# Two-stage attention and a squared-ReLU MLP on one core: a seventh group of seven-product block multiplies, products added inside PSUM, weight differences moved to GpSimd

## The chip, the cores and the metric

The kernel runs on one core of one Trainium2 chip. The core's engines run side by side and meet at semaphores: TensorE (PE in the profile; PEld is its weight loads), VectorE (DVE), ScalarE (ACT), GpSimd (POOL) and SyncE (SP). Each engine works through its own list of instructions in order. Matrix products land in PSUM; DVE and ACT carry them from there to SBUF. The metric is the time of one execution on the device in microseconds, taken as the median of several runs.

## The reference

For each of 8 batches and 8 heads there are 576 tokens of 64 numbers (q, k, v) and 32 pack vectors p. Two attentions follow one another, and an MLP takes the heads of a token side by side as 512 numbers:

```python
def sm_attn(qq, kk, vv):
    s = scale * np.matmul(qq, kk.transpose(0, 1, 3, 2))
    s = s - np.max(s, axis=-1, keepdims=True)
    a = np.exp(s)
    a = a / (np.sum(a, axis=-1, keepdims=True) + 1e-09)
    return np.matmul(a, vv)
p_packed = sm_attn(p, k, v)
out = sm_attn(q, p_packed, p_packed)
...
x = np.ascontiguousarray(attn_out.transpose(0, 2, 1, 3)).reshape(B * S, H * D)
h = x @ w_in          # 4608 x 512 times 512 x 2048
r = np.maximum(h, 0.0)
return ((r * r) @ w_out).astype(np.float32)   # 4608 x 2048 times 2048 x 512
```

## The kernel before, in words

**Stages of a batch.** For batch b the kernel transposes k (Tk), forms the pack scores on PE (S1), takes their maxima on DVE (MX) and exponentials on ACT (EX), transposes them (E, EC) and multiplies with v (PV). The packed vectors are normalised (RC, XN) and, instead of being carried through the second attention, multiplied with w_in first: four products M of 512 columns each, copied to SBUF by MC. The second attention's scores come from S2; SI transposes them, SM, SU, SE, SS, SN and SO are its softmax (maxima, subtraction, exponential, sum, scaling, transposition). F1 (for batches 0 and 1 cut in pieces, F) multiplies the probabilities with M and gives h transposed, 128 of its 2048 features at a time; R takes the ReLU out of PSUM, SQ (or Q) squares it into the tile `gT`.

**The last product.** `gT` holds the squared values of two batches. The product with w_out runs over tiles of 128 tokens, numbered 0 to 35. A plain tile (F2, lines 907 to 911) is 16 matmuls of 512 columns that add up in one PSUM bank, one copy (FC) and a store (ST). Where four whole tiles lie in a batch, they can be a group: 512 tokens times 2048 features times 512 columns is cut into 2 by 2 blocks, and seven block products replace eight. Groups exist for batches 2 to 7. Each product GP.z.g (z = 0 to 6, group g, two halves of eight matmuls of 256 columns, line 975) needs block sums: GS.0 to GS.3 are sums of squared values for each group (line 963), WS.0 to WS.3 differences of blocks of w_out, made once (line 956, two halves each, so 8 instructions of 1,024 columns). The seven products take turns in two PSUM banks (`OUTS`); GC carries them to the output tile `o_sb`: one copy and seven additions that read `o_sb` and PSUM (line 994).

**What sets the order.** A planner written in the kernel (`Plan.forward`) lists every piece of work with its engine, its length and what it needs, and lays the pieces out by priorities. A table of numbers, found by search, shifts the priorities (`TABLE`, 'o') and the choice between ACT and DVE (`TABLE`, 'l'), so that the order of each engine's list is fixed when the program is built. Before the first F2, PE's gaps are filled with products of a zero tile that nobody reads (`keep_clock`, line 590). Inputs are loaded by POOL's DMA queue in the order of the string `ORDER`; each load waits until the eighth load before it has landed (line 1018). Batches 5, 6 and 7 are transposed by DMA from SP's queue once the loads are through; SP also issues nearly all stores.

The pieces that the change touches: GROUPS (line 223), `w_sum` (952), `gp_mm` (967), `g_copy` and `g_add` (987, 991), the GC list (from 1253), the WS pieces (1230), and the tile 'e1T' that EC and the DMA transposes write.

Of the kernel before, what the change touches and what calls it, by code (L numbers as in the profile page):

```python
# [41 lines left out]
class Plan:  # L42
# [6 lines left out]
    def add(self, *a, **kw):  # L49
        self.pieces.append(Piece(*a, **kw))  # L50
# [169 lines left out]
ORDER = "k0 v0 x0 a0 y0 a1 a2 a3 k1 b0 b1 v1 b2 q1 b3 b4 b5 b6 b7 k2 v2 q2 k3 v3 q3 k4 v4 q4 k5 v5 q5 k6 v6 q6 k7 v7 q7"  # L220

KHW = 2
GROUPS = (2, 3, 4, 5, 6, 7)
XBAR = (5, 6, 7)

TABLE = {'o': {'Lk.0.0i': -10.9333, 'Lk.0.1i': -54.9223, 'Lk.0.0': 47.5347, 'LP.0': -80.9731, 'Lk.0.1': -9.0183, 'I2':
# [270 lines left out]
def kernel_impl(tc, q, k, v, p, w_in, w_out, out):  # L497
# [23 lines left out]
    with ExitStack() as ctx:  # L521
# [213 lines left out]
        def s1_tr(b, qd, u):  # L735
            t = pst[b, qd] = half(u[0]).bitcast(BF16)[:, :(GM + 1) * P]
            for g in range(GM + 1):
                c0 = g * P if g < GM else S - P
                nc.tensor.transpose(t[:, g * P:(g + 1) * P], e1[:, qd, c0:c0 + P], ident[:])
# [615 lines left out]
```

## Time and profile before

| | before |
|---|---|
| median of 3 runs | 237.85 us (237.77 to 238.49) |
| the profiled execution | 238.34 us, of which the span of its instructions is 236.6 us |
| PE busy | 225.6 us, 95% of the span |
| DVE busy | 202.5 us, 86% |
| ACT busy | 157.2 us, 66% |
| POOL busy | 59.2 us, 25%, all but one instruction of it in the first 113 us |
| granted PE clock over the span | 0.99 |

PE's busy time is 95% over the whole span, but that is an average over parts that differ: a beginning in which PE waits for loads and a chain of softmax steps, a long middle in which it hardly pauses, and an end that is the last copy and store. DVE is nearly as full as PE between 40 and 200 us. The profiled execution took 238.34 us, 0.49 us more than the median, so sums that are made against it are carried over to the median as differences.

### The profile page before, as it was taken

Reading aid. Unit: us, or ns where it says so; the run is one execution under the profiler, and the core shown is the slowest. Engines: PE = TensorE matmul, PEld = TensorE weight load, DVE = VectorE, ACT = ScalarE, POOL = GpSimd, SP = SyncE. Lnnn points to the kernel's source line nnn. Section 1 sums busy time; section 2 is a strip of 40 time slices with the busy share of each in tenths; the row PEclk is TensorE's granted clock in tenths of the full one; section 3 lists DMA queues with packets and bytes.
Section 4 is the critical chain, followed back from the end, with each engine's and each line's share of the span. In section 5 each row is a group of like instructions: output and inputs, shape, how many; then the busy total and the mean of one; then the engine's idle time right before and its main releaser. Section 6 shows DMA issues by size and latency. Waiting matters only on the chain.

```text
span 236.6 us, 6395 instructions
## 1 busy us (share of the span) xinstructions
PE 225.6 (95%) x2636; PEld 160.2 (68%) x2636; DVE 202.5 (86%) x340; ACT 157.2 (66%) x245; POOL 59.2 (25%) x106
## 2 busy tenths in 40 slices
PE   8888899999999999999999999999999999999991
PEld 5556655346544457857788877777848888888880
DVE  3669977997989999999998889999999999849550
ACT  3314987279959889899787834766977999516000
POOL 9787555333344657600000000000000000000000
PEclk9979999999999999999999999999999999999999
DMA  7999999999999999957596989738501003305216
GB/s 228 173 194 182 205 209 202 201 198 260 229 212 219 214 237 198 197 75 144 94 126 144 183 97 195 169 59 157 125 3 44 3 1 89 91 0 131 71 22 177
DMA packets 46764, 34.06 MB, mean 144 GB/s; under 512 B 25392, under 2 KB 38448, under 8 KB 46736
## 3 DMA queue, kind: packets, MB, share of 16 engines
q0 software_dynamic: 19408, 17.90, 47.2%
q1 hardware_dynamic: 26496, 14.98, 29.5%
q10 hardware_dynamic: 832, 0.79, 1.1%
q8 instruction: 20, 0.33, 0.6%
q14 instruction: 8, 0.07, 0.1%
HBM read 37.22 MB, written 9.44 MB: 197 GB/s over the span
## 4 chain that ended last, share of the span: by engine, by line
PE 82%; DVE 12%; ACT 2%; issue 1%; ACTq 1%; DVEq 0%
PE pb L975 31%; PE ps L857 20%; PE pb L911 8%; PE ps L885 6%; PE ps L911 4%; PE ps L783 3%; PE pb L590 2%; PE ps L706 1%; DVE wS L956 1%; PE ps L800 1%; DVE s L821 1%; ACTq L923 1%; ACT e L733 1%; DVE m L827 1%; DVE s L831 1%
## 5 line engine op out<-in xcount | busy, mean ns | idle before, releaser
L867 ACT ACTIVATE r_b<-ps 128x576 bf16<-128x576 f32 x80 | 46.8, 672 | 14.8 <-PE ps L857 14.2
L857 PE MATMUL ps<-a,M 128*128 128x288 bf16 x384 | 52.7, 286 | 0.0
L857 PEld LDWEIGHTS <-M 128*128 128x128 bf16 x384 | 37.2, 98 | 9.9 <-issue 0.2
L975 PEld LDWEIGHTS <-gT 128*128 128x128 bf16 x384 | 37.2, 98 | 6.4 <-issue 1.1
L584 ACT CAST M<-ps 128x1024 bf16<-128x1024 f32 (+1 forms) x33 | 29.8, 945 | 16.3 <-PE ps L783 16.2
L994 DVE TENSOR_TENSOR o_sb<-o_sb,pb 128x512 f32<-128x512 f32 x42 | 28.0, 676 | 8.3 <-PE pb L975 7.4
L911 PE MATMUL pb<-w_out_b,gT 128*128 128x512 bf16 x128 | 34.3, 380 | 0.1
L975 PEld LDWEIGHTS <-gS 128*128 128x128 bf16 x288 | 27.5, 98 | 5.5 <-issue 1.9
L923 POOL DMA_DIRECT2D out_dram<-o_sb x1 | 0.6, 577 | 118.7 <-issue 118.7
L911 PEld LDWEIGHTS <-gT 128*128 128x128 bf16 x176 | 15.8, 98 | 17.5 <-issue 4.0
L875 ACT ACTIVATE gT<-r_b 128x1152 bf16<-128x1152 bf16 x21 | 24.2, 1176 | 0.4 <-DVE r_b L869 0.2
L975 PE MATMUL pb<-wS,gS 128*128 128x256 bf16 x192 | 24.0, 273 | 0.0
L975 PE MATMUL pb<-wS,gT 128*128 128x256 bf16 x192 | 23.6, 273 | 0.0
L975 PE MATMUL pb<-w_out_b,gT 128*128 128x256 bf16 x192 | 23.6, 273 | 0.0
L893 ACT ACTIVATE r_b<-ps 128x512 bf16<-128x512 f32 (+2 forms) x27 | 16.8, 654 | 6.5 <-PE ps L885 6.5
L877 DVE TENSOR_TENSOR gT<-r_b 128x1152 bf16<-128x1152 bf16 x27 | 19.6, 747 | 1.6 <-ACT r_b L867 1.6
L885 PE MATMUL ps<-a,M 128*128 128x256 bf16 (+3 forms) x160 | 18.9, 262 | 1.9 <-DVE a L848 0.9
L885 PEld LDWEIGHTS <-M 128*128 128x128 bf16 x160 | 13.9, 97 | 6.8 <-issue 2.6
L584 ACT COPY o_sb<-pb 128x512 f32<-128x512 f32 (+1 forms) x14 | 7.9, 565 | 15.1 <-PE pb L929 12.6
L733 ACT ACTIVATE e<-ps,n 128x576 bf16<-128x576 f32 x16 | 11.8, 738 | 8.4 <-DVE n L725 7.0
L590 PE MATMUL pb<-zero 128*128 128x256 bf16 x92 | 15.2, 332 | 1.1 <-DVE zero L593 1.1
L834 ACT ACTIVATE e<-s 128x1152 bf16<-128x1152 f32 (+4 forms) x11 | 10.1, 917 | 7.0 <-DVE s L831 6.9
(92 smaller groups left out, 341.4 us busy)
## 6 DMA issues: line engine op xcount, KB each, us to landing
out_dram<-o_sb SPq DMA_DIRECT2D x65, 128.0 KB, 2.6
kq_b<-in_k_dram POOLq DMA_DIRECT2D x14, 288.0 KB, 10.1
kq_b<-in_q_dram POOLq DMA_DIRECT2D x10, 288.0 KB, 6.1
w_in_b<-in_moe_w_in_dram POOLq DMA_DIRECT2D x16, 128.0 KB, 5.7
w_out_b<-in_moe_w_out_dram POOLq DMA_DIRECT2D x8, 256.0 KB, 9.2
v_b<-in_v_dram POOLq DMA_DIRECT2D x5, 320.0 KB, 10.5
v_b<-in_v_dram POOLq DMA_DIRECT2D x12, 128.0 KB, 8.2
v_b<-in_v_dram POOLq DMA_DIRECT2D x5, 256.0 KB, 11.0
```

Of the source, the lines that this page charges most:

```text
L584: nc.scalar.copy(dst, src)
L590: nc.tensor.matmul(half(7)[:, :2 * P], lhsT=zero[:, :P], rhs=zero, start=True, stop=True)
L733: nc.scalar.activation(e_out(qd) if b in XBAR else e1[:, qd, :S], ps1[b, qd], ACT.Exp, bias=n1[b % 2][:, qd:qd + 1], accum_out=d1[b % 2][: ...
L857: nc.tensor.matmul(t[:, c], lhsT=M[b % 2][:, qd, fb * FB:(fb + 1) * FB], rhs=a2[b % 2][:, qd, c * HALF:(c + 1) * HALF], start=(qd == 0), s ...
L867: nc.scalar.activation(dst, src, ACT.Relu)
L875: nc.scalar.activation(dst, r, ACT.Square)
L877: eng.tensor_tensor(out=dst, in0=r, in1=r, op=ALU.mult)
L885: nc.tensor.matmul(t[:, c, m * w:(m + 1) * w], lhsT=M[b % 2][:, qd, fb * FB:(fb + 1) * FB], rhs=a2[b % 2][:, qd, o:o + w], start=(qd == 0) ...
L893: nc.scalar.activation(dst, ph["h", b, x, j], ACT.Relu)
L911: nc.tensor.matmul(po[t], lhsT=gT[:, fb, n0:n0 + P], rhs=w_out_b[:, fb, :], start=(fb == 0), stop=(fb == NFB - 1))
L975: nc.tensor.matmul(pz[g, k][:, i], lhsT=a[:, f, i * P:(i + 1) * P], rhs=w[:, f], start=(h == 0 and f == 0 and i == 0), stop=(h == 1 and f ...
L994: nc.vector.tensor_tensor(out=oC(g, i, j), in0=oC(g, *src), in1=pz[g, z], op=op)
```

## The change

- `GROUPS` gets batch 1: tiles 5, 6, 7 and 8 become a group of seven products in place of four plain tiles. Tiles 0 to 4, 13, 22 and 31 stay plain.
- Products 2, 3, 5 and 6 of a group no longer start a new sum in a PSUM bank. They add to the bank that already holds product 0, 1, 3 or 4 (`ON`), after GC has read it. The bank's readers so become two copies (GC.0, GC.2) and five additions in place of one copy and seven additions. The sign of WS.3 is turned around so that all of them add.
- The eight differences WS go from DVE to POOL, into the queue that issues the loads: two by two they stand behind the first load of q for batch 2 (four), between the two loads of k for batch 4 and behind the second (two), and among the loads of batch 4's q and behind batch 5's k (two).
- `e1T` becomes part of the tile `e1`, and the zero tile of `keep_clock` lies in a slot of `o_sb`.
- The table of priorities is a new one throughout, so the order of all engines' lists is another; PE's list has 112 matmuls of 256 columns more, 64 of 512 columns less, and 92 fillers as before.
- New tokens in `ORDER`, `XTURN` and `quiet` change nothing with the values given; the planner's lengths for the DMA transposes go from 2.0 and 3.4 to 1.6 and 2.9.

```diff
-GROUPS = (2, 3, 4, 5, 6, 7)
+GROUPS = (1, 2, 3, 4, 5, 6, 7)
 XBAR = (5, 6, 7)
+XTURN = (5, 6, 7)
...
-        zero = consts.tile([P, 2 * P], BF16, name="zero")
...
-        e1f = consts.tile([P, NQD * (GM + 1) * P + D], BF16, name="e1")
+        e1f = consts.tile([P, 2 * NQD * (GM + 1) * P], BF16, name="e1")
...
-        e1T = consts.tile([P, NQD, GM + 1, P], BF16, name="e1T")
+        e1T = e1f[:, NQD * (GM + 1) * P:].rearrange("p (q g n) -> p q g n", q=NQD, n=P)
...
+        zero = o_sb[:, 0, :P].bitcast(BF16)
...
-            a, b = ((wB(0, 1, hs), wB(0, 0, hs)), (wB(1, 1, hs), t[0]), (wB(1, 1, hs), wB(0, 1, hs)), (t[1], wB(1, 0, hs)))[i]
-            nc.vector.tensor_tensor(out=t[i], in0=a, in1=b, op=ALU.subtract)
+            a, b = ((wB(0, 1, hs), wB(0, 0, hs)), (wB(1, 1, hs), t[0]), (wB(1, 1, hs), wB(0, 1, hs)), (wB(1, 0, hs), t[1]))[i]
+            nc.gpsimd.tensor_tensor(out=t[i], in0=a, in1=b, op=ALU.subtract)
...
+        ON = {2: 0, 3: 1, 5: 3, 6: 4}
         def gp_mm(g, k, h, u=None):
-            if u is not None:
-                pz[g, k] = half(u[0]).rearrange("p (i n) -> p i n", i=2)
+            if h == 0:
+                pz[g, k] = pz[g, ON[k]] if k in ON else half(u[0]).rearrange("p (i n) -> p i n", i=2)
...
-                                     start=(h == 0 and f == 0 and i == 0), stop=(h == 1 and f == HB // 2 - 1 and i == 1))
+                                     start=(k not in ON and h == 0 and f == 0 and i == 0), stop=(h == 1 and f == HB // 2 - 1 and i == 1), skip_group_check=k in ON)
...
-                add(f"WS.{i}.{h}", [("DVE", 0.6, lambda i=i, h=h: w_sum(i, h))],
+                add(f"WS.{i}.{h}", [("POOL", 2.3, lambda i=i, h=h: w_sum(i, h))],
...
             for z in range(7):
+                seen = [f"GC.{ON[z]}.{g}"] if z in ON else []
...
-            add(f"GC.0.{g}", either(lambda g, eng, u: g_copy(g, 1, 0, 0, eng, u), 0.485, 0.6, g), [f"GP.0.{g}.1"], take=[OP], free=[(f"GP.0.{g}.0", 0)], level=L - 50)
-            for z, i, j, src, bank, op, after in ((1, 0, 1, (1, 0), 1, ALU.add, (0,)), (2, 0, 0, (1, 0), 2, ALU.add, (1,)), (3, 1, 0, (0, 1), 3, ALU.add, (1, 2)),
-                                                  (4, 1, 1, (1, 0), 4, ALU.add, (3,)), (5, 0, 1, (0, 1), 4, ALU.add, (3,)), (6, 1, 0, (1, 0), 5, ALU.subtract, (4,)),
-                                                  (7, 0, 1, (0, 1), 6, ALU.add, (5,))):
...
+            last = {2: 0, 5: 1, 6: 4}
+            for z, i, j, src, after in ((0, 1, 0, None, ()), (1, 0, 1, (1, 0), (0,)), (2, 0, 0, None, (1,)), (3, 1, 1, (1, 0), (0,)), (4, 1, 1, (1, 1), (3,)),
+                                        (5, 1, 0, (1, 0), (1, 3)), (6, 0, 1, (0, 1), (1,))):
+                if src is None:
+                    how = either(lambda g, i, j, z, eng, *u: g_copy(g, i, j, z, eng, *u), 0.485, 0.6, g, i, j, z)
+                else:
+                    how = [("DVE", 0.61, lambda *u, g=g, i=i, j=j, src=src, z=z: g_add(g, i, j, src, z, *u))]
```

More of the change, by code (lines that the diff above doesn't have):

```diff
@@ L985, in o_take, with g_copy, g_add @@
                 ob[first(g) + 2 * i + x] = o_sb[:, o + x]
-        def g_copy(g, i, j, z, eng, u):
-            o_take(g, i, u)
-            cast(eng, oC(g, i, j), pz[g, z])
-        def g_add(g, i, j, src, z, op=ALU.add, u=None):
+        def g_copy(g, i, j, z, eng, u=None):
             if u is not None:
                 o_take(g, i, u)
-            nc.vector.tensor_tensor(out=oC(g, i, j), in0=oC(g, *src), in1=pz[g, z], op=op)
+            cast(eng, oC(g, i, j), pz[g, z])
+        def g_add(g, i, j, src, z, u=None):
+            if u is not None:
+                o_take(g, i, u)
+            nc.vector.tensor_tensor(out=oC(g, i, j), in0=oC(g, *src), in1=pz[g, z], op=ALU.add)
         plan = Plan()
@@ L1031, in kernel_impl @@
             add("I2", [("POOL", 2.1, setup2)], line="load", level=-250)
+        quiet, pending = {}, []
         for x in ORDER.split():
             n = int(x[1:])
-            if x[0] in "kqxy":
+            if x[0] == "p":
+                quiet[n] = issued[-1:]
+                pending += [f"T{nm}.{n}.{qd}" for nm in "kq" for qd in QDS] + [f"PX.{i}" for i in range(2) if n == X0]
+            elif x[0] in "kqxy":
                 for qd in QDS:
@@ L1074, in kernel_impl @@
             add(f"P.{i}", [("DVE", 0.07 + (b1 - b0) * 0.066, lambda i=i, b0=b0, b1=b1: p_cast(i, b0, b1))], [f"LP.{i}"], level=10.0 * i - 9.5)
-            add(f"PT.{i}", [("DVE", 0.07 + (min(b1, X0) - b0) * 0.066, lambda b0=b0, b1=b1: p_tr(b0, min(b1, X0)))], [f"P.{i}"], level=10.0 * i - 9.5)
+            if b0 < X0:
+                add(f"PT.{i}", [("DVE", 0.07 + (min(b1, X0) - b0) * 0.066, lambda b0=b0, b1=b1: p_tr(b0, min(b1, X0)))], [f"P.{i}"], level=10.0 * i - 9.5)
         for qd in range(KHW):
@@ L1102, in over @@
             return [f"{kind}.{nm}" for nm, o1, w1, _ in (steps(b - 1) if b else ()) if o < o1 + w1 and o1 < o + w]
-        quiet = [f"L{ORDER.split()[-1][0]}.{B - 1}.{x}" for x in range(2)]
         if XBAR:
             for i in range(2):
-                add(f"PX.{i}", [("SP", 1.5, lambda i=i: xbar_p(i))], ["P.2"] + (["P.1"] if X0 == 2 else []) + quiet, lag=3.4, level=-5)
+                add(f"PX.{i}", [("SP", 1.5, lambda i=i: xbar_p(i))], ["P.2"] + (["P.1"] if X0 == 2 else []) + quiet.get(X0, issued[-1:]), lag=XLAG, level=-5)
         for b in range(B):
@@ L1113, in kernel_impl @@
                 if b in XBAR:
-                    add(f"Tk.{b}.{qd}", [("SP", XUS, lambda b=b, qd=qd: xbar(kT, "k", b, qd))], [f"Lk.{b}.{qd}", f"S1.{b - 1}"] + quiet[:1 + (b > 5)], lag=XLAG, level=L - 20)
+                    add(f"Tk.{b}.{qd}", [("SP", XUS, lambda b=b, qd=qd: xbar(kT, "k", b, qd))], [f"Lk.{b}.{qd}", f"S1.{b - 1}"] + quiet.get(b, issued[-2:-1] if b == X0 else issued[-1:]), lag=XLAG, level=L - 20)
                     continue
@@ L1132, in kernel_impl @@
                 add(f"EX.{b}.{qd}", [("ACT", 0.76, lambda b=b, qd=qd: s1_exp(b, qd))],
-                    [f"MX.{b}.{qd}"] + ([f"E.{b - 1}" + ("" if b - 1 in XBAR else f".{qd}")] if b else []) + ([f"RC.{b - 2}"] if b > 1 else []), free=[(s1, hold)], level=L + 1)
-                if b in XBAR:
+                    [f"MX.{b}.{qd}"] + ([f"E.{b - 1}" + ("" if b - 1 in XTURN else f".{qd}")] if b else []) + ([f"RC.{b - 2}"] if b > 1 else []), free=[(s1, hold)], level=L + 1)
+                if b in XTURN:
                     if qd:
@@ L1141, in kernel_impl @@
                     free=[(f"E.{b}.{qd}", 0)], level=L + 1)
-            add(f"PV.{b}", [("PE", 0.5, lambda u, b=b: pv_mm(b, u))], [*([f"E.{b}"] if b in XBAR else [f"EC.{b}.0", f"EC.{b}.1"]), *([f"Lv.{b}.{i}" for i in range(6)] + [f"VZ.{b}"] if b in XBAR else [f"Lv.{b}.0", f"Lv.{b}.1"])] + (["I2"] if b else []),
+            add(f"PV.{b}", [("PE", 0.5, lambda u, b=b: pv_mm(b, u))], [*([f"E.{b}"] if b in XTURN else [f"EC.{b}.0", f"EC.{b}.1"]), *([f"Lv.{b}.{i}" for i in range(6)] + [f"VZ.{b}"] if b in XBAR else [f"Lv.{b}.0", f"Lv.{b}.1"])] + (["I2"] if b else []),
                 line="PV", take=[ONES[:3] if b < 2 else ONES], mode=2, level=L + 1)
@@ L1165, in kernel_impl @@
                 elif b in XBAR:
-                    add(f"Tq.{b}.{qd}", [("SP", XUS, lambda b=b, qd=qd: xbar(qT, "q", b, qd))], [f"Lq.{b}.{qd}"] + s2n + quiet, lag=XLAG, level=L - 20)
+                    add(f"Tq.{b}.{qd}", [("SP", XUS, lambda b=b, qd=qd: xbar(qT, "q", b, qd))], [f"Lq.{b}.{qd}"] + s2n + quiet.get(b, issued[-1:]), lag=XLAG, level=L - 20)
                 else:
@@ L1248, in kernel_impl @@
             for z in range(7):
+                seen = [f"GC.{ON[z]}.{g}"] if z in ON else []
                 for h in range(2):
-                    add(f"GP.{z}.{g}.{h}", [("PE", 0.875, (lambda u, g=g, z=z: gp_mm(g, z, 0, u)) if h == 0 else lambda g=g, z=z, h=h: gp_mm(g, z, h))],
-                        need[z][h], line="GP", take=[OUTS] if h == 0 else (), level=L, key=f"GP.{z}.{g}")
-            add(f"GC.0.{g}", either(lambda g, eng, u: g_copy(g, 1, 0, 0, eng, u), 0.485, 0.6, g), [f"GP.0.{g}.1"], take=[OP], free=[(f"GP.0.{g}.0", 0)], level=L - 50)
@@ L1254, in kernel_impl @@
-            for z, i, j, src, bank, op, after in ((1, 0, 1, (1, 0), 1, ALU.add, (0,)), (2, 0, 0, (1, 0), 2, ALU.add, (1,)), (3, 1, 0, (0, 1), 3, ALU.add, (1, 2)),
-                                                  (4, 1, 1, (1, 0), 4, ALU.add, (3,)), (5, 0, 1, (0, 1), 4, ALU.add, (3,)), (6, 1, 0, (1, 0), 5, ALU.subtract, (4,)),
-                                                  (7, 0, 1, (0, 1), 6, ALU.add, (5,))):
-                fn = lambda *u, g=g, i=i, j=j, src=src, bank=bank, op=op: g_add(g, i, j, src, bank, op, *u)
-                add(f"GC.{z}.{g}", [("DVE", 0.61, fn)], [f"GP.{bank}.{g}.1"] + [f"GC.{x}.{g}" for x in after], take=[OP] if z == 1 else (),
-                    free=[(f"GP.{bank}.{g}.0", 0)], level=L - 50)
+                    add(f"GP.{z}.{g}.{h}", [("PE", 0.875, (lambda u, g=g, z=z: gp_mm(g, z, 0, u)) if h == 0 and z not in ON else lambda g=g, z=z, h=h: gp_mm(g, z, h))],
+                        need[z][h] + seen, line="GP", take=[OUTS] if h == 0 and z not in ON else (), level=L, key=f"GP.{z}.{g}")
@@ new lines, in kernel_impl @@
+            last = {2: 0, 5: 1, 6: 4}
[5 more added lines that the diff above has]
+                    how = [("DVE", 0.61, lambda *u, g=g, i=i, j=j, src=src, z=z: g_add(g, i, j, src, z, *u))]
+                add(f"GC.{z}.{g}", how, [f"GP.{z}.{g}.1"] + [f"GC.{x}.{g}" for x in after], take=[OP] if z < 2 else (),
+                    free=[(f"GP.{last[z]}.{g}.0", 0)] if z in last else [], level=L - 50)
```

19 lines of the change are left out of this document (11 added, 8 removed), and 536 rows, old and new, of the table TABLE.

## The prediction

> **What bounds the kernel now.** I read the page first (busy times, slices, chain), then the chain in order of time, then busy time by stage.
>
> ```profile
> span 236.6 us, 6395 instructions
> PE 225.6 (95%) x2636; PEld 160.2 (68%) x2636; DVE 202.5 (86%) x340; ACT 157.2 (66%) x245; POOL 59.2 (25%) x106
> ...
> DVE  3669977997989999999998889999999999849550
> ...
> PE 82%; DVE 12%; ACT 2%; issue 1%; ACTq 1%; DVEq 0%
> ```
>
> The chain that ends last runs on PE for 82% of the span, on DVE for 12%. So work taken from PE is worth its length, but only where DVE does not become the later of the two; the slices show DVE at nine tenths from 40 to 200 us. The stages decide (columns: start and end, length, then busy time of PE, PEld, DVE, ACT, POOL):
>
> ```profile
> 40.90:51.90 11.00, 10.45 (x97) 4.18 (x96) 10.82 (x20) 5.85 (x8) 4.08 (x7) 1.00 1.23 198
> 51.90:65.10 13.20, 13.14 (x94) 8.34 (x93) 11.09 (x23) 12.12 (x21) 4.12 (x8) 1.00 1.17 240
> 65.10:86.00 20.90, 20.48 (x374) 9.35 (x373) 19.49 (x32) 16.00 (x28) 11.71 (x21) 1.00 1.22 219
> 86.00:192.70 106.70, 106.68 (x1277) 80.58 (x1275) 102.59 (x149) 83.90 (x128) 9.92 (x18) 1.00 0.66 118
> 192.70:231.40 38.70, 38.70 (x347) 33.65 (x344) 28.57 (x45) 16.66 (x21) 0.31 (x1) 1.00 0.27 67
> ```
>
> 40.9 us is batch 1's S2, 51.9 the first F of batch 1, 65.1 batch 2's S1, 86.0 batch 2's first F1, 192.7 batch 7's. In the first and third stage DVE is as full as PE; in the last it has 10 us free. The granted clock is 1.00 in all.
>
> **The change, part by part.**
>
> *PE.* The program's lists show 64 matmuls of 512 columns fewer and 112 of 256 columns more.
>
> ```profile
> 78.77 2.59 PE ps L911 x12
> ...
> 217.41 10.62 PE pb L975 x96
> ...
> 105.05 0.77 PE ps L783 x24
> ...
> 120.31 2.45 PE ps L857 x20
> ```
>
> In the chain 12 wide ones take 2.59 us (0.216 each) and 96 narrow ones 10.62 (0.111; 0.109 elsewhere in the chain). 64 x 0.216 = 13.8 goes, 112 x 0.109 = 12.2 comes: **-1.6 us**, and no more than that can come from the seventh group itself. A product that adds to its bank waits for the copy or addition that reads it; another product of 16 x 0.109 = 1.7 us lies between, longer than a 0.68 us addition, so I cost that wait at nothing. In the tail group 7's seven products follow one another unbroken but for one half tile, and DVE has the room.
>
> *DVE and ACT.*
>
> ```profile
> L994 DVE TENSOR_TENSOR o_sb<-o_sb,pb 128x512 f32<-128x512 f32 x42 | 28.0, 676 | 8.3 <-PE pb L975 7.4 <-ACT r_b L867 0.4 <-DMA out_dram<-o_sb 0.2
> L963 DVE TENSOR_TENSOR gS<-gT,gS 128x1024 bf16<-128x1024 bf16 x12 | 8.2, 683 | 1.0 <-PE pb L975 0.9
> L956 DVE TENSOR_TENSOR wS<-w_out_b 128x1024 bf16<-128x1024 bf16 x4 | 2.6, 668 | 0.0
> L869 DVE TENSOR_SCALAR r_b<-ps 128x576 bf16<-128x576 f32 x16 | 11.4, 742 | 1.0 <-PE ps L857 0.8 <-ACT r_b L867 0.2
> L877 DVE TENSOR_TENSOR gT<-r_b 128x1152 bf16<-128x1152 bf16 x27 | 19.6, 747 | 1.6 <-ACT r_b L867 1.6
> L867 ACT ACTIVATE r_b<-ps 128x576 bf16<-128x576 f32 x80 | 46.8, 672 | 14.8 <-PE ps L857 14.2 <-DVE gT L877 0.5
> L875 ACT ACTIVATE gT<-r_b 128x1152 bf16<-128x1152 bf16 x21 | 24.2, 1176 | 0.4 <-DVE r_b L869 0.2
> ```
>
> By the lists DVE loses 7 additions (-4.7) and 8 differences (-5.3), gains 8 group sums (+5.4), gives 11 ReLUs to ACT (-8.2) and takes 14 squares (+10.5): -2.3 in all. ACT takes the ReLUs (+7.4) and gives the squares (-16.5), and three copies more go to it (some +1.7): -7.4. After 86 us this loosens both; of the 2.5 us by which that stage's 106.7 exceeds its PE work (104.2 us, its pieces by the list at the spacings above, F1's four matmuls at 4/20 of 2.45), I take 0.5 as gained: **-0.5**.
>
> *Where group 1 lands.* Its products stand right behind batch 2's S1, in place of the plain tiles that filled PE there. PE's list to that point is 3 wide matmuls shorter (-0.65), but three F pieces of batch 0 move from ahead of its last softmax step to behind it:
>
> ```profile
> 24.73 2.17 PE ps L885 x24
> ```
>
> These 24 matmuls (2.17 us) ran where PE waits anyway. Bounds 0 and +2.2; I take +0.7, a third, since the pieces put in their place start as soon as the softmax step ends. Together **0** at 65.1 us (bounds -0.7 and +1.5). From there to batch 2's first F1 DVE's list is the same but for four additions of GC, two group sums, one transposition (0.8) and a small one more, and two differences and one copy of `e1T` (0.5) fewer: 4 x 0.68 + 2 x 0.68 + 1.0 - 2 x 0.67 - 0.5 = 3.2 us. It had 19.49 busy in 20.9. With overlaps of neighbours (some 0.07 each) 22.3 us are needed: **+1.4** on that stage (bounds +1.1 and +3.2). What is left for PE behind it is less by 9 wide matmuls (-1.9) and two M pieces of 0.26 (-0.5), plus one transposition (+0.3): **-2.2**, which holds the -1.6.
>
> *The differences on POOL.* The trace has no arithmetic of two operands on POOL. The nearest rows:
>
> ```profile
> L662 POOL MEMSET v_b<- 32x512 bf16 x6 | 3.1, 517 | 0.2
> ...
> 88.46 1.32 DVE L831 TENSOR_TENSOR s<-s,m 128x1152 f32<-128x1152 f32 x1
> ...
> 111.78 1.35 DVE L831 TENSOR_TENSOR s<-s,m 128x1152 f32<-128x1152 f32 x1
> ...
> 88.85 1.07 POOL L662 MEMSET v_b<- 32x512 bf16 x2
> ```
>
> A memset writes 512 in 0.52 us, so 1,024 in 1.03. Two reads and a write take between one such pass and three; I take two, 2.07 us each, 16.6 for eight. The Trainium skill, page "GPSIMD Engine Reference", section "3.1 Elementwise — side-by-side cycle accounting", gives 4497 ns for 2,048 elements; by half of that, an estimate, the eight would take 18.0.
>
> What they do to DVE is the open price. Below: nothing, as for the memset at 88.85, beside which the DVE subtraction took 1.32 us against 1.35 with POOL idle. But a memset reads nothing, while these read the memory from which DVE takes both its operands. Above: each holds back a DVE instruction of two operands for its whole 2.07 us. The first four stand here:
>
> ```profile
> 41.42 0.56 POOL L632 DMA_DIRECT2D kq_b<-in_q_dram  x1 [0.63 <-DMA w_out_b<-in_moe_w_out_dram]
> 42.93 0.53 POOL L634 DMA_DIRECT2D kq_b<-in_q_dram  x1 [0.95 <-DVE m L827]
> ...
> 43.51 0.65 DVE L831 TENSOR_TENSOR s<-s,m 128x512 f32<-128x512 f32 x1
> ...
> 46.00 0.82 DVE L831 TENSOR_TENSOR s<-s,m 128x640 f32<-128x640 f32 x1
> ...
> 48.77 0.78 DVE L844 TENSOR_TENSOR n<-e,r 128x256 bf16<-128x256 bf16 x2
> ```
>
> Four in a row fill 42.0 to 50.3. The first would hold the subtraction at 43.5 for 0.5; the second the next one for up to 2.1; a third or fourth the scaling at 48.8 for up to 2.1: between 0.5 and 4.7, half is 2.5, or 0.64 each. Batch 1's F waits at the end of this very list, and PE's cover there is its 35 wide matmuls and four M pieces (7.6 + 1.0 = 8.6) against DVE's 8.3: 0.3. So **+2.2**. Three more differences fall in the next stage (1.9), where PE has 13.7 us of work against DVE's list of 12.0: 1.6 of cover, **+0.3**. The last two fall in the stage where DVE is already late: **+1.3**. Sum +3.8; with no hold 0, with every hold at 2.07 (8.3 - 0.3, 6.2 - 1.6, 4.1) +16. I take the middle of a hold since the traces have neither; one that DVE mostly misses is as likely as one that it mostly meets.
>
> The Trainium skill, page "SBUF — State Buffer", section "Who interferes with whom", states that a DVE instruction with two SBUF inputs contends with a GpSimd instruction that reads SBUF, and that the first to start blocks the other to its end. By it the price is above 0, and DVE's own instructions hold POOL too. No run here shows it yet; against the memset rows it makes no claim, since those only write.
>
> *POOL's queue.* The loads behind the first four differences leave 8.3 us later. The second half of q for batch 2, issued at 42.93, then leaves at about 50.8:
>
> ```profile
> kq_b<-in_q_dram POOLq DMA_DIRECT2D x8, 144.0 KB, 10.8
> ...
> 59.98 0.77 DVE L675 STREAM_TRANSPOSE qT<-kq_b 128x576 f32<-128x576 f32 x1
> ```
>
> Its landing took 10.8 us behind a full queue, so 61.6 at the latest; its transposition ran at 59.98 and stands behind one more group sum now. Eight loads are under way when POOL leaves, so I cost this at nothing, with a bound of +2.
>
> *The tail.*
>
> ```profile
> 229.60 1.91 PE L929 MATMUL pb<-w_out_b,gT 128*128 128x256 bf16 x16
> 231.56 0.37 ACT L584 COPY o_sb<-pb 128x256 f32<-128x256 f32 x1 [11.52 <-PE pb L929]
> ```
>
> The same half tile 31, copy and store end the new list: nothing.
>
> **Sum.** 0 + 1.4 - 2.2 - 0.5 + 3.8 = +2.5 us on the profiled 238.34 is 240.8; on the median 237.85, 240.4.
>
> **The rivals.**
> - *No hold* (faster): POOL's reads cost DVE nothing. Then -1.3, 236.6 us, in a range of 235.2 to 238.3 by the bounds of the two early stages. For it speak the memset rows; against it only that both engines read. It decides below 0.27 us per difference: by the covers above 6 x 0.27 - 0.3 is the 1.3 us of the gain.
> - *DVE late without any hold*: the stage after 65.1 costs its full +3.2 and nothing is won after 86 us: 237.85 + 3.2 - 2.2 = 238.9. For it: 19.49 us of 20.9 are busy there already.
> - *Products wait for POOL*: product 1 of group 1 needs WS.1, which stands behind a k load that was issued at
>
> ```profile
> 57.23 0.56 POOL L632 DMA_DIRECT2D kq_b<-in_k_dram  x1 [0.81 <-DVE wS L956]
> ```
>
> If that is late by the whole 7.4 us that the first four add beyond the 0.9 us of waiting that they replace, WS.1's two halves end at 64.6 + 0.6 + 2.1 + 0.5 + 2.1 = 69.9, against 65.1 + 2.6 = 67.7 needed: 2.2 us on top of the forecast, 242.6.
>
> **How the numbers follow.** A measurement of this kernel tells 0.3% (0.7 us) from no change. Chances: the forecast 0.46 (its own range 238.6 to 243), no hold 0.36, DVE late 0.10, products wait 0.08. Faster holds no hold but for its upper end, 0.32; same, 237.1 to 238.6, gets 0.03 of that and 0.04 of DVE late; slower is the rest, 0.61. The range, 235.6 to 244.0, leaves out the low end of no hold and holds met at nearly every difference.
>
> **What would show it.** Right: DVE's subtractions and scalings between 42 and 54 us longer than 0.65 to 0.82, or gaps before them, while POOL's line of `w_sum` is busy, and PE idle before batch 1's first F, released by DVE's `a`. Wrong: those DVE rows as before, batch 2's S1 by 65 us and PE unbroken to the end. The stage sum is wrong if batch 2's F1 starts less than 21 us behind its S1, the queue's price if PE waits on `wS` or DVE on a load.

## The result, and the profile after

The changed kernel is slower: 5.3% over the kernel before, by a ratio of 1.053 with a 95% interval of 1.0489 to 1.057. With before at 238.17 us in the same session that is 250.8 us; the forecast was 240.4, in a range of 235.6 to 244.0. Its four executions took 250.17, 251.47, 255.25 and 255.5 us: 250.8 stands for the two shorter ones, and the profiled one is one of the longer (255.25 us, span 253.5), so its rows show where the time goes, but their amounts are those of an execution 17 us over before.

The head of its page and two of its slices:

```profile
span 253.5 us, 6508 instructions
PE 229.7 (91%) x2684; PEld 167.5 (66%) x2684; DVE 215.3 (85%) x338; ACT 149.0 (59%) x244; POOL 76.6 (30%) x115
...
PE   8897896097899889999999999999999999999992
...
PEclk9979799769799999999999999999999999999999
```

PE is down from 95% to 91% of a longer span. One slice of PE, at 44 to 51 us, reads 0, and the granted clock falls there and right behind; from 95 us on PE is full again. The stages, cut at batch 2's S1, its first F1 and PE's last matmul (columns as in the prediction):

```profile
79.70:104.50 24.80, 22.20 (x445) 15.51 (x445) 24.01 (x37) 17.60 (x29) 18.68 (x29) 1.00 1.09 169
104.50:249.00 144.50, 143.63 (x1602) 113.55 (x1599) 126.93 (x184) 91.94 (x148) 7.10 (x13) 1.00 0.54 99
```

S1 stands at 79.7 us in place of 65.1 (+14.6), the stage behind it takes 24.8 in place of 20.9 (+3.9), and the rest 144.5 in place of 145.5 (-1.0). So the loss of this execution lies ahead of 104 us, most of it ahead of 80, where POOL does the first six differences. The waits of PE name DVE (columns: what waited for what, us in total, times, longest):

```profile
PE ps L913 <- DVE ppT L588: 8.2, 1, 8.2
PE ps L887 <- DVE a L850: 3.1, 2, 2.2
```

And these are DVE's and POOL's rows in order of time (start, length, engine, line, what; the lines are some two higher than before: L958 is `w_sum`, L907 the squares of batch 1, L833 the subtraction of the maxima, L846 the scaling, L965 the group sums):

```profile
41.98 8.34 POOL L958 TENSOR_TENSOR wS<-w_out_b 128x1024 bf16<-128x1024 bf16 x4
...
60.01 2.14 POOL L958 TENSOR_TENSOR wS<-w_out_b,wS 128x1024 bf16<-128x1024 bf16 x1
...
83.45 2.16 POOL L958 TENSOR_TENSOR wS<-w_out_b,wS 128x1024 bf16<-128x1024 bf16 x1
```

```profile
42.10 8.64 DVE L907 TENSOR_TENSOR gT<-r_b 128x768 bf16<-128x768 bf16 x1 [0.84 <-ACT r_b L895]
50.66 0.21 DVE L588 COPY ppT<-ps 128x128 bf16<-128x128 bf16 x1
...
58.54 0.76 DVE L839 TENSOR_REDUCE t<-e 128x20 f32<-128x640 bf16 x1
...
59.53 4.06 DVE L846 TENSOR_TENSOR n<-e,r 128x256 bf16<-128x256 bf16 x4
...
83.84 2.32 DVE L965 TENSOR_TENSOR gS<-gT,gS 128x1024 bf16<-128x1024 bf16 x1
```

One square of 768 elements takes 8.64 us: it begins 0.12 us behind POOL's first subtraction and ends 0.4 us behind its fourth. The four scalings take 4.06 us where they take 1.53 in a run below, and a group sum 2.32 in place of 0.68. The reduction at 58.54 runs beside a subtraction (57.36 to 59.50) in its usual 0.76: it reads one operand. Over their usual lengths (0.56, 1.53, 0.68) the three rows hold 8.1 + 2.5 + 1.6 = 12.2 us. POOL's eight subtractions together take 16.9.

DVE's list is in order, so behind the held square stand the copy of `ppT`, which the four M products need, and the squares themselves are what the plain tiles wait for. PE therefore stood still for 8.16 us at once; the profile names the copy, which ends 0.13 us behind the square, as what released the plain tile. Two of POOL's eight subtractions held nothing: beside those at 57.36 and 79.21 DVE had reductions, transpositions and other rows of its usual lengths.

### The profile page after: what moved, and what is told of

Same layout as the page of the kernel before. It is cut to its first block, busy times and chain, and to the rows that moved or that the text cites. A ratio compares the mean times of both kernels' runs of the same rounds, so it can differ in the third digit from the quotient of the medians.

```text
span 253.5 us, 6508 instructions
## 1 busy us (share of the span) xinstructions
PE 229.7 (91%) x2684; PEld 167.5 (66%) x2684; DVE 215.3 (85%) x338; ACT 149.0 (59%) x244; POOL 76.6 (30%) x115
## 4 chain that ended last, share of the span: by engine, by line
PE 53%; DVE 6%; ACT 3%; DMA 1%; issue 1%; SPq 1%; DVEq 0%; ACTq 0%
PE pb L980 29%; PE ps L859 16%; PE pb L913 3%; PE ps L785 2%; DVE gT L879 2%; PE pb L931 1%; ACT r_b L869 1%; DVE o_sb L1000 1%; DMA out_dram<-o_sb 1%; DVE gS L965 1%; PE ps L802 1%; DVE s L826 1%; ACT e L586 1%; SPq L925 1%; DVE qT L677 1%
## 5 line engine op out<-in xcount | busy, mean ns | idle before, releaser
L869 ACT ACTIVATE r_b<-ps 128x576 bf16<-128x576 f32 x91 | 52.4, 667 | 8.4 <-PE ps L859 8.4
L980 PEld LDWEIGHTS <-gS 128*128 128x128 bf16 x336 | 32.1, 98 | 6.8 <-issue 1.6
L1000 DVE TENSOR_TENSOR o_sb<-o_sb,pb 128x512 f32<-128x512 f32 x35 | 23.7, 677 | 11.8 <-PE pb L980 11.1
L879 DVE TENSOR_TENSOR gT<-r_b 128x1152 bf16<-128x1152 bf16 x41 | 30.3, 749 | 2.1 <-ACT r_b L869 2.0
L980 PE MATMUL pb<-w_out_b,gT 128*128 128x256 bf16 x224 | 28.1, 273 | 0.0
L980 PE MATMUL pb<-wS,gT 128*128 128x256 bf16 x224 | 27.8, 273 | 0.4 <-DVE o_sb L1000 0.4
L980 PE MATMUL pb<-wS,gS 128*128 128x256 bf16 x224 | 27.6, 273 | 0.4 <-DVE gS L965 0.4
L895 ACT ACTIVATE r_b<-ps 128x512 bf16<-128x512 f32 (+2 forms) x25 | 15.7, 652 | 12.0 <-PE ps L887 11.9
L913 PE MATMUL pb<-w_out_b,gT 128*128 128x512 bf16 x80 | 21.5, 379 | 0.0
L907 DVE TENSOR_TENSOR gT<-r_b 128x512 bf16<-128x512 bf16 (+2 forms) x18 | 16.1, 916 | 2.2 <-ACT r_b L895 2.1
L913 PE MATMUL ps<-w_out_b,gT 128*128 128x512 bf16 x32 | 9.5, 446 | 8.5 <-DVE ppT L588 8.2
```

The costliest lines, as they stand in the source:

```text
L869: nc.scalar.activation(dst, src, ACT.Relu)
L879: eng.tensor_tensor(out=dst, in0=r, in1=r, op=ALU.mult)
L895: nc.scalar.activation(dst, ph["h", b, x, j], ACT.Relu)
L907: eng.tensor_tensor(out=dst, in0=r, in1=r, op=ALU.mult)
L913: nc.tensor.matmul(po[t], lhsT=gT[:, fb, n0:n0 + P], rhs=w_out_b[:, fb, :], start=(fb == 0), stop=(fb == NFB - 1))
L980: nc.tensor.matmul(pz[g, k][:, i], lhsT=a[:, f, i * P:(i + 1) * P], rhs=w[:, f], start=(k not in ON and h == 0 and f == 0 and i == 0), sto ...
```

## The experiments

**Where the loss sits.** The first four runs leave one cause in or out at a time. Three theories: H, the subtractions hold DVE; Q, POOL's queue lets the loads leave too late; R, the seventh group and the new order are slower themselves.

The differences back on DVE, all else as changed:

```diff
-            nc.gpsimd.tensor_tensor(out=t[i], in0=a, in1=b, op=ALU.subtract)
+            nc.vector.tensor_tensor(out=t[i], in0=a, in1=b, op=ALU.subtract)
```

> The changed kernel with its eight weight differences issued on DVE, at the places of the plan, and nothing else changed. Theory H (a POOL subtraction holds DVE's two-operand instructions, and a run of them holds one for the whole run) and theory Q (the loads behind the subtractions leave too late, above all behind WS.3, which waits for P.2 at the head of POOL's queue) both take all the loss from POOL: some 236 to 240 us, since DVE gets 8 x 0.67 = 5.3 us of work back and the rest of the change was forecast at -1.3. Theory R (the new order and the seventh group themselves cost the time) expects 246 or more. By H or Q the DVE square that took 8.64 us takes 0.6 and PE's gap at 45 to 50 us is gone.

Measured: 241.98 us, ratio 1.017 (1.013 to 1.021). Most of the loss is gone, so R is out as the main cause, but the time is 2 us over the upper end of what H and Q expected: the eight differences cost this order 241.98 - 238.90 = 3.1 us on DVE, against the next run, which has them on neither engine.

Writes in place of the differences:

```diff
-            nc.gpsimd.tensor_tensor(out=t[i], in0=a, in1=b, op=ALU.subtract)
+            for _ in range(2):
+                nc.gpsimd.memset(t[i], 0.0)
```

> The changed kernel with two POOL memsets of the same 1,024 elements in place of each subtraction: some 2.1 us of POOL at the same places of its queue, the same wait for P.2, but nothing read. It leaves the differences out, so the products of the groups are wrong. H: no hold, the square between 42 and 51 us takes 0.6, and some 8 of the 13 us come back, 239 to 243. Q: POOL is as late as before, 248 to 251. A middle result divides the loss between the two.

Measured: 238.90 us, ratio 1.0033 (1.0006 to 1.006). Its rows:

```profile
43.58 7.69 POOL L959 MEMSET wS<- 128x1024 bf16 x8
...
59.42 1.98 POOL L959 MEMSET wS<- 128x1024 bf16 x2
```

```profile
42.48 0.56 DVE L907 TENSOR_TENSOR gT<-r_b 128x768 bf16<-128x768 bf16 x1 [0.84 <-ACT r_b L895]
...
45.74 1.42 DVE L833 TENSOR_TENSOR s<-s,m 128x512 f32<-128x512 f32 x2
...
50.08 1.53 DVE L846 TENSOR_TENSOR n<-e,r 128x256 bf16<-128x256 bf16 x4
```

POOL is as busy at the same places (7.69 us against 8.34), and the two f32 subtractions and the scalings beside it take what they always take. So the queue's delay costs next to nothing, and what the subtractions add to it, 250.8 - 238.9 = 11.9 us, comes from their reading and what follows from it. That is H. The 12.2 us of held DVE time in the trace are near to it, but they are no second measurement of the same thing: they belong to the execution of 255.25 us, which is 16.4 us over 238.9, and no trace of a shorter one was kept. Where the other 4 us of that execution went isn't shown.

The stall in POOL's queue, which the forecast had not seen: WS.3 overwrites the tile that P.2 reads, and in the changed kernel it stood 15.15 us at the head of the queue with the second half of q for batch 4 and the loads of batch 5 behind it. The page names no releaser, but P.2 ends at 79.06:

```profile
78.51 0.55 DVE L619 TENSOR_SCALAR p_b<-wS 128x768 bf16<-128x768 f32 x1
```

```profile
79.21 2.12 POOL L958 TENSOR_TENSOR wS<-w_out_b,wS 128x1024 bf16<-128x1024 bf16 x1 [15.15 <-issue]
```

```diff
-            p_f.append(wS[:, 3].rearrange("p a n -> p (a n)")[:, :(B - 2) * 2 * NQD * D].bitcast(F32))
...
+        p_f.append(o_sb[:, 0:2].rearrange("p a n -> p (a n)")[:, P:P + (B - 2) * NQD * D])
```

> The changed kernel with the input of P.2 in two free slots of o_sb in place of wS[3], so that WS.3 has nothing to wait for; the order is the same. H: the hold at 42 to 50 us stays, POOL's 15.15 us of idle time before WS.3.0 goes and the loads behind it leave up to 15 us earlier; that gives 1 to 4 us, 247 to 250. Q: most of the loss was that stall, 240 to 243. If the loads were early enough all the same: 250 to 251.

Measured: 252.69 us, ratio 1.0594 (1.0558 to 1.0631): nothing won. In the profiled execution (259.29 us, where the other four took 252.16 to 253.15) the stall is gone (WS.3 runs at 63.46), but now it meets the scalings of batch 1, and four of them take 6.98 us:

```profile
58.99 6.98 DVE L846 TENSOR_TENSOR n<-e,r 128x256 bf16<-128x256 bf16 x4
```

Q's 240 to 243 is out, so the stall, 15.15 us long, was not the loss. H's 247 to 250 missed too; the scalings are a likely reason, seen in that one execution.

The other way round, the kernel before with only its differences on POOL (`nc.vector` to `nc.gpsimd` in its line 956):

> The kernel before with its eight differences issued on POOL at their old places in the plan, where loads stand between most of them, and nothing else changed. H, with the hold lasting only until POOL's run of subtractions ends: single holds of up to 2.1 us and one pair of 4.2; DVE loses 5.3 us of its own work; 239 to 245. No hold between separated subtractions: 236 to 239. Q: the loads are later by up to 2.1 us for each difference ahead of them, which they can bear while seven others are on the way: 237 to 239.

Measured: 244.87 us, ratio 1.0264 (1.0226 to 1.0303): 6.5 us for one word. DVE's rows at the first differences, and POOL's:

```profile
43.48 4.35 DVE L831 TENSOR_TENSOR s<-s,m 128x512 f32<-128x512 f32 x1
47.75 0.81 DVE L827 TENSOR_REDUCE m<-s 128x20 f32<-128x640 f32 x1
48.59 2.01 DVE L831 TENSOR_TENSOR s<-s,m 128x640 f32<-128x640 f32 x1
```

```profile
43.07 4.20 POOL L956 TENSOR_TENSOR wS<-w_out_b 128x1024 bf16<-128x1024 bf16 x2
47.20 0.55 POOL L634 DMA_DIRECT2D kq_b<-in_q_dram  x1
47.77 2.13 POOL L956 TENSOR_TENSOR wS<-w_out_b,wS 128x1024 bf16<-128x1024 bf16 x1
```

The rows that took 0.65 and 0.82 take 4.35 and 2.01. The seventh group is not needed for the loss.

**What holds, and what ends it.** One operand in place of two on POOL:

```diff
-            nc.gpsimd.tensor_tensor(out=t[i], in0=a, in1=b, op=ALU.subtract)
+            nc.gpsimd.tensor_copy(t[i], a)
```

> The changed kernel with a POOL copy of the same 1,024 elements in place of each subtraction: one operand is read from SBUF instead of two, the places are the same. It leaves the differences out, so the products of the groups are wrong. If any read by POOL holds DVE's two-operand work: the square at 42 us is held as long as the four copies run, some 4 to 8 us, and the time is 244 to 251. If the hold needs POOL to read two operands: the square takes 0.6, and the time is that of the memsets, 238 to 240.

Measured: 241.9 us, ratio 1.0148 (1.0112 to 1.0184), between the two.

```profile
42.32 3.00 POOL L958 COPY wS<-w_out_b 128x1024 bf16<-128x1024 bf16 x3
```

```profile
44.17 1.70 DVE L833 TENSOR_TENSOR s<-s,m 128x512 f32<-128x512 f32 x1
```

A copy reads one operand and holds too: the f32 subtraction at 44.17 ends 0.55 us behind the third copy (45.32), 1.70 us in place of 0.65. So one operand that POOL reads is enough for a hold. The price is a quarter of that of the subtractions (241.9 - 238.9 = 3.0 us in place of 11.9), while a copy takes half as long as a subtraction (1.05 us to 2.12). The square had also passed before the first copy; no run divides the difference between the two.

Loads between the first four subtractions:

```diff
+        for n, x in (("WS.2.0", "Lq.2.1.0i"), ("WS.0.1", "Lq.2.1.1i"), ("WS.2.1", "Lk.3.0i")):
+            at[n] = at[x] + 0.001
...
+        for p in sorted(out, key=lambda p: at[p.name]):
```

> The changed kernel with a load's issue between each two of the first four subtractions; the order is the same otherwise. Theory H-run: a hold lasts as long as POOL goes on without a gap, so here it is cut into holds of at most 2.1 us, and between them and during them DVE gets its one-operand instructions done; as in the kernel before with its differences on POOL, about 1.4 us are lost per subtraction, not 2.1: some 3 us come back, 246 to 249. Theory H-each: each subtraction holds whatever two-operand instruction meets it, and DVE has one ready nearly always: 250 to 252.

Measured: 250.07, 254.4, 254.81 and 255.57 us, which is the span of the changed kernel's own executions (250.17 to 255.5): no gain to be seen.

```profile
42.32 2.14 POOL L961 TENSOR_TENSOR wS<-w_out_b 128x1024 bf16<-128x1024 bf16 x1
44.38 0.56 POOL L639 DMA_DIRECT2D kq_b<-in_q_dram  x1
44.95 2.13 POOL L961 TENSOR_TENSOR wS<-w_out_b 128x1024 bf16<-128x1024 bf16 x1
...
50.25 2.13 POOL L961 TENSOR_TENSOR wS<-w_out_b 128x1024 bf16<-128x1024 bf16 x1
```

```profile
43.66 9.28 DVE L836 TENSOR_TENSOR s<-s,m 128x512 f32<-128x512 f32 x1
```

One f32 subtraction of 0.65 us waited through four of POOL's and the three load issues between them. A gap of 0.5 us was not enough to let it in, though it was in the kernel before with its differences on POOL, above. With a longer gap, a memset of 0.97 us ahead of each of the first four:

```diff
+            if i in (0, 2):
+                nc.gpsimd.memset(t[i], 0.0)
             nc.gpsimd.tensor_tensor(out=t[i], in0=a, in1=b, op=ALU.subtract)
```

> The changed kernel with a POOL memset of the same 1,024 elements (0.97 us) ahead of each of the first four subtractions, so that POOL goes 1 us without reading between two of them; the queue behind them is 3.9 us later. If a held DVE instruction gets in when POOL stops reading for long enough (the 0.5 us of a load's issue were too short in all four gaps of the run with loads between): the 8.6 us of the square become at most 2.7, each later hold at most 2.1, one-operand work runs beside the subtractions, and 1 to 4 us come back, 247 to 250. If it stays held through memsets too: 12 us or more in one instruction, 253 to 256.

Measured: 248.22 us, ratio 1.0426 (1.0388 to 1.0464), as the first case expected.

```profile
43.31 2.12 POOL L960 TENSOR_TENSOR wS<-w_out_b 128x1024 bf16<-128x1024 bf16 x1
45.38 0.94 POOL L959 MEMSET wS<- 128x1024 bf16 x1
46.40 2.30 POOL L960 TENSOR_TENSOR wS<-w_out_b 128x1024 bf16<-128x1024 bf16 x1
```

```profile
43.70 3.01 DVE L833 TENSOR_TENSOR s<-s,m 128x512 f32<-128x512 f32 x2
```

The held instruction gets in when the memset starts, and the second one runs beside it: 3.01 us for the two, where the first alone had waited 9.28. With 3.9 us more in POOL's queue the kernel is still 2.6 us faster.

**Parts of the price.** The first four on DVE, the last four on POOL:

```diff
-            nc.gpsimd.tensor_tensor(out=t[i], in0=a, in1=b, op=ALU.subtract)
+            (nc.vector if i in (0, 2) else nc.gpsimd).tensor_tensor(out=t[i], in0=a, in1=b, op=ALU.subtract)
```

> The changed kernel with WS.0 and WS.2 (the first four differences) on DVE and WS.1 and WS.3 on POOL, at the places of the plan. By the holds in the trace of the changed kernel the first four cost 8.1 of 12.1 us and the last four 4.0; DVE pays 4 x 0.68 = 2.7 for the first four. Theory H: 250.8 - 8.1 + 1.6 (half of the 3.1 us by which eight on DVE stand above none) = 244 to 245. If the clock and the wait for P.2 that follow from the first hold were a loss of their own, less: 242 to 243. If the last four were as dear as the first: 247 or more.

Measured: 246.87 us, ratio 1.0364 (1.0333 to 1.0394), 2 us over what H said and next to the third case, 247 or more. The last four are dearer than they were behind a stage that was late already: here the first two of them (58.15 to 62.94) meet a square that takes 5.23 us, through a load's issue between.

```profile
58.06 5.23 DVE L907 TENSOR_TENSOR gT<-r_b 128x640 bf16<-128x640 bf16 x1
```

So the holds don't add up place by place: what one group of differences costs depends on where DVE's list stands when they come, and the group ahead of them shifts that.

The clock. PE lost its clock in and behind the 8 us gap (columns: stretch, length, busy time of PE, PEld, DVE, ACT, POOL, then the granted clock):

```profile
45.00:50.00 5.00, 0.00 (x0) 0.00 (x0) 5.00 (x1) 0.00 (x0) 5.00 (x3) 0.77 1.23 191
50.00:55.00 5.00, 4.07 (x11) 1.51 (x11) 4.86 (x8) 0.63 (x1) 4.40 (x8) 0.54 1.19 206
```

The first try filled the gap with products into a PSUM tile whose other columns DVE still had to read:

```diff
+            if p.name == "F2.2.6":
+                self.keep(64, 1)
...
```

> The changed kernel with 64 filler matmuls of 128 columns in PE's gap behind the last scores of batch 1 (43 to 50 us), so that PE does not stand idle while DVE is held. If the fall of the granted clock behind that gap (0.54 in 50 to 55 us, where 14 wide matmuls take 4.96 us instead of 3.0) is a part of the loss of its own: 1 to 3 us come back, 248 to 250, and the clock in 50 to 55 us is 1.00. If the stage waits for DVE all the same: 250 to 252.

Measured: 251.05 us, ratio 1.0537 (1.0492 to 1.0582). It says little, since DVE's transposition of the scores now waited 3.07 us for the fillers, and the clock in 50 to 55 us was still 0.72. The second try adds zero into banks that are open anyway, and nobody waits for it:

```diff
+            n = {"F2.2.6": 70, "F.1.0.0": 18}.get(p.name, 0)
+            if n:
+                self.keep(n, 6)
...
-        def keep_clock(n):
+        def keep_clock(n, z=7):
             for _ in range(n):
-                nc.tensor.matmul(half(7)[:, :2 * P], lhsT=zero[:, :P], rhs=zero, start=True, stop=True)
+                nc.tensor.matmul(half(z)[:, :2 * P], lhsT=zero[:, :P], rhs=zero, start=z == 7, stop=z == 7)
```

> The changed kernel with fillers that add zero into a bank that is open anyway: 70 of 256 columns in PE's 8.2 us gap behind the last scores of batch 1, and 18 ahead of batch 1's first F. They wait for nothing and nobody waits for them, so only PE's idleness goes. Theory C (the idle PE loses its clock, and the slower clock behind it is a loss of its own): the 14 wide matmuls behind the gap take 3.0 us instead of 4.96, the clock in 50 to 55 us is 0.9 or more, and the time is 247 to 249, with no runs at 255. Theory H alone: the stage waits for DVE, 250 to 252.

Measured: 252.83 us in the median (250.72 to 254.99), ratio 1.0596 (1.0514 to 1.0678). Its clock and the rows of the same place:

```profile
50.00:55.00 5.00, 5.00 (x51) 1.78 (x49) 4.03 (x6) 2.54 (x4) 4.43 (x8) 1.00 1.18 204
```

```profile
48.76 3.18 PE L916 MATMUL ps<-w_out_b,gT 128*128 128x512 bf16 x14
```

```profile
43.77 7.14 DVE L836 TENSOR_TENSOR s<-s,m 128x512 f32<-128x512 f32 x1
```

The clock is whole and the 14 wide matmuls take 3.18 us in place of 4.96, and the time is no better. So the fall of the clock, which came with the hold, shows no cost of its own; theory C's 247 to 249 is out. A small cost isn't ruled out, for the fillers are work too, and what was held this time is another instruction, the f32 subtraction: the square had got through, 0.9 us ahead of POOL.

That led to the last question on the hold, whether it is a race at 42 us that makes some executions longer. One memset ahead of the first subtraction alone:

```diff
+            if (i, h) == (0, 0):
+                nc.gpsimd.memset(t[i], 0.0)
             nc.gpsimd.tensor_tensor(out=t[i], in0=a, in1=b, op=ALU.subtract)
```

> The changed kernel with one POOL memset (0.97 us) ahead of the first subtraction alone, so that the square that started 0.12 us behind the subtraction in the profiled run (42.10 against 41.98) goes ahead of it in every run. If the executions of the changed kernel at 255 us are those in which that square is caught, with PE standing at once, and those at 250 to 251 those in which it gets through and the f32 subtraction behind it is caught instead (as in the run with zero fillers, 7.14 us): all executions lie within 249 to 252. If the two kinds come from something else: some at 254 to 256 again.

Measured: 248.48 us, ratio 1.0436 (1.04 to 1.0473); six executions from 245.84 to 249.68, none at 254 or more. That fits the race, but six against four are few, and the run with loads between, whose profiled execution took 255.57 us, has a free square in that very trace (0.56 us, at 40.40), as has the run with zero fillers, with executions at 253.72 and 254.99. So a caught square is not needed for a long execution, and the race isn't shown. The time is better than either expectation, and in its profile (245.84 us) the held instructions got in between subtractions that follow without a gap, which they hadn't in the changed kernel:

```profile
42.88 9.38 POOL L960 TENSOR_TENSOR wS<-w_out_b 128x1024 bf16<-128x1024 bf16 x4
```

```profile
43.47 4.74 DVE L833 TENSOR_TENSOR s<-s,m 128x512 f32<-128x512 f32 x2
```

POOL pays for it: its four take 9.38 us in place of 8.34.

**What moving is worth without the hold.** Memsets in place of the differences, in the kernel before:

```diff
-            nc.vector.tensor_tensor(out=t[i], in0=a, in1=b, op=ALU.subtract)
+            for _ in range(2):
+                nc.gpsimd.memset(t[i], 0.0)
```

> The kernel before with two POOL memsets of the same 1,024 elements in place of each of its eight differences. It leaves the differences out, so the products of the groups are wrong. It shows what the eight differences cost DVE in the kernel before, 8 x 0.67 = 5.3 us of busy time, and so what moving them is worth if nothing is held. If DVE sets the pace of the stages where they stand (40.9 to 65.1 us and the next): 1.5 to 4 us faster, 234 to 237, and then the seventh group and the new order lose 2 to 4 us against the forecast, since the changed kernel with memsets took 238.9. If PE covers them: 237.5 to 238.5, and the forecast of the rest was too good by about 2 us.

Measured: 237.99 us, ratio 1.0002 (0.9981 to 1.0022). The three stages by the boundaries of the forecast:

```profile
40.90:51.90 11.00, 10.51 (x92) 4.42 (x84) 8.88 (x17) 5.61 (x8) 9.29 (x12) 1.00 1.23 197
51.90:65.10 13.20, 13.03 (x99) 8.19 (x107) 9.26 (x19) 12.52 (x22) 10.56 (x16) 1.00 1.18 242
65.10:86.00 20.90, 19.64 (x362) 9.52 (x353) 19.03 (x31) 15.88 (x29) 14.94 (x25) 1.00 1.21 220
```

DVE has 8.88, 9.26 and 19.03 us of work in place of 10.82, 11.09 and 19.49, 4.2 us less in all, and the time is the same. No gain was eaten by later loads: between 40.9 and 86 us PE's longest wait is 0.44 us, for a copy on DVE, and none of those listed is for a load. PE covered the differences. The kernel before paid nothing for them on DVE, so in its order there was nothing to be had by moving them; the new order, above, pays 3.1 us. Of the versions after the change that compute the differences the one with all of them on DVE is the fastest, 241.98 us, and still 1.7% over before.

## Why the prediction was wrong

The direction and the mechanism were right, the size was not, and the range ended 6.8 us below the result. By the runs the 12.6 us over before (250.8 - 238.2) divide into 11.9 for the differences on POOL, where the forecast had 3.8, and 0.7 for all the rest, where it had -1.3.

*The differences on POOL: the step that failed.* The length of one was right (2.07 forecast, 2.12 to 2.16 in the rows). The price was "the middle of a hold", 0.64 us each, since "one that DVE mostly misses is as likely as one that it mostly meets". By the trace six of the eight met a two-operand instruction and held it to their end: 12.2 us, or 1.5 for each of the eight. Two things in the working made it small. It asked which rows of the kernel before would fall on the slots of the subtractions, as if each met DVE by chance. But DVE had work nearly all the time (10.82 of 11.0 us), and with an in-order list a hold seldom misses: DVE goes on through its one-operand rows until it comes to a two-operand one, and stands there. And it held that a hold lasts one subtraction; four in a row, with 0 to 0.5 us between, held one instruction for 8.64 us, and with loads between for 9.28. The working also has a slip: four, three and two differences make nine, where there are eight. In the runs it is four, two and two, and with the same covers that gives +3.5 in place of +3.8, and with every hold at 2.07 us 8.0 + 2.5 + 4.1 = +14.6, where the recorded terms, 8.0, 4.6 and 4.1, add up to 16.7 and are called +16. The slip is not what failed: the 11.9 lie within either bound, and the range left out "holds met at nearly every difference", which is what came.

*The cover.* It is a part of the same step. PE was given 8.6 us of cover there, 35 wide matmuls and four M products. PE waited 8.16 us all the same, because these need what DVE makes: the M products the copy of `ppT`, which stands right behind the held square, and the plain tiles the squares. Cover counts only where the covering work doesn't wait for the engine that is late. The place that the forecast named, PE idle before batch 1's first F by DVE's `a`, is the smaller wait (2.24 us of the 3.1 in the row above).

*The rule on the two engines.* The Trainium skill, page "SBUF — State Buffer", section "Who interferes with whom", says that a DVE instruction with two SBUF inputs contends with a GpSimd instruction that reads SBUF, not with one that only writes. The traces agree: the square took 8.64 us beside subtractions and 0.56 beside memsets, and a reduction with one operand 0.76 as ever. On how long the loser waits the measurement goes further than the page's "whole instruction": one DVE instruction took 9.28 us, through four instructions of POOL.

*POOL's queue, at nothing with a bound of +2*: no cost shows. The memsets put nearly the same time into the queue, and the whole kernel is then 0.3% over before; in the kernel before they change nothing (1.0002). The wait of WS.3 for P.2 was missed in the working, and did no harm that shows: without it the time was 252.69.

*Products wait for POOL.* In the profile of the changed kernel PE waits for no `wS`. The wait for a bank's reader, which was costed at nothing, is 0.4 us there in all, so that step held.

*No hold, and DVE late without any hold.* The memset run is the case without a hold, and it came out at 238.9, where the first of these rivals said 236.6 (235.2 to 238.3) and the second 238.9. Its windows, cut at batch 2's S1 and first F1 (66.1 and 89.6 us) and PE's end:

```profile
66.10:89.60 23.50, 22.14 (x444) 15.45 (x444) 22.55 (x37) 17.59 (x29) 16.74 (x28) 1.00 1.19 206
89.60:234.10 144.50, 143.40 (x1598) 113.58 (x1600) 126.99 (x184) 91.94 (x149) 9.59 (x18) 1.00 0.62 106
```

The stage that was 20.9 us took 23.5, +2.6 against a forecast of +1.4 (bounds +1.1 and +3.2), with DVE busy for 22.55 of it. Behind it 145.5 us became 144.5: -1.0 against -2.7. S1 stood at 66.1 in place of 65.1. These are rows of an execution that took 240.58 us, so their sum is 1.7 us above the median, and the first of the three may be chance. So the -1.6 us of PE work did not turn into time. The work on DVE and ACT was mis-sized as well: DVE's busy time is 203.5 us in place of 202.5, where the count of lists said -2.3, and ACT's 148.2 in place of 157.2, where it said -7.4. Among what the count leaves out on DVE are two more ReLUs of 640 elements and two more copies of M. The second rival had the right sum for this part, 238.9, but by other parts (+3.2 and -2.2 in place of +1.0, +2.6 and -1.0 there), so the agreement is partly luck.

*DVE's relief after 86 us, -0.5.* The relief came, but nothing speaks for a gain: behind batch 2's first F1 the memset run has 126.99 us of DVE work in place of 131.16, and the time there fell by less than the PE work alone was to give. Taking eight differences from DVE in the kernel before, ahead of 86 us, gained 0 too (0.9981 to 1.0022), though DVE was at nine tenths there.

*The tail, nothing*: right; it ends on the same half tile, 0.37 us of copy behind the last matmul.

## What to carry to other kernels

Work that moves to GpSimd is not off VectorE's path if it reads SBUF: while it reads, VectorE's instructions with two SBUF operands can be held, and with them all that is behind them in its list. Before moving, count how much of VectorE's list there has two operands, and where VectorE is nearly full reckon with up to the mover's whole length (16.9 us of subtractions cost 11.9 here, and some 17 us of them 6.5 in the kernel before). If it must be, leave a microsecond without a read between two instructions, which gave 2.6 us back here, or put them where VectorE has only reductions, transpositions and copies from PSUM. And test by substitution before building on it: memsets in place of the moved work told in one run that there was nothing to gain in the old order (1.0002), and in another what the reading cost (11.9 us).

## What the runs showed of the hardware that was not expected

- A held VectorE instruction need not get its turn at the end of the GpSimd instruction that holds it. In the changed kernel, in the run with zero fillers and in the one with its own tile for P.2 it waited through a run without gaps; with loads between it waited through three gaps of 0.5 us, too, and in the run of the kernel before with differences on POOL it got in at a gap of the same length. In the run with one memset ahead it got in without any gap. What decides isn't settled; a gap of 1 us, in one run, sufficed both times that one was waiting.
- Starting first didn't help: a scaling that began at 59.53, 0.48 us ahead of POOL's subtraction at 60.01, and takes 0.43 us on its own, took 2.92. Here POOL's recorded start may be late.

```profile
59.53 2.92 DVE L846 TENSOR_TENSOR n<-e,r 128x256 bf16<-128x256 bf16 x1
```

- A GpSimd copy with a single operand holds as well (1.70 us for an instruction of 0.65), and where VectorE gets in GpSimd waits in turn (9.38 us for four subtractions in place of 8.34).
- PE's clock fell to 0.54 behind a gap of 8 us, and with zero products that kept it at 1.00 the kernel was no faster: the engine that was late was another.
